# A fused attention and Mish block on one NeuronCore: emission pair by pair on three double PSUM slots, roots on GpSimd, residual seeded into PSUM, smaller first loads

## The chip, the cores and the metric

The kernel runs on one core of one Trainium2 chip. The metric is device time in microseconds (us), the median of several executions; the kernel before takes 204.78 us (204.29 to 205.15 in three runs). The profiler gives a span a little shorter than that time (202.8 us in a run of 204.61 us); all the stage arithmetic below is in the span of the profiled run.

TensorE (PE) multiplies, VectorE (DVE) does statistics, softmax normalisation and half of the casts, ScalarE (ACT) does exponentials, Mish and copies, GpSimd (POOL) has little to do, and SyncE (SP) issues most DMAs. "PEclk" and "clock" are the share of full speed that the throttle granted TensorE.

## The reference

One token block of 2048 x 512. A layernorm feeds two branches: a Hedgehog linear attention (32 heads of 16, feature map by two softmaxes, not causal) and a dense pair with Mish. The sum of the input and both branches is the output.

```python
x  = A_x                                   # 1 x 2048 x 512, bf16
xn = (x - mean) / sqrt(var + 1e-5)
q, k, v = split_heads(xn @ wqkv)           # 32 heads of 16
phi(q)  = concat(softmax(q @ w_phi), softmax(-q @ w_phi))
phi(k)  = concat(softmax(k @ w_phi), softmax(-k @ w_phi))
kv = sum_s phi(k) v ;  z = sum_s phi(k)    # over all 2048 tokens
o  = (phi(q) @ kv) / (phi(q) . z + 1e-6)
h  = xn @ w1 + b1                          # 512 -> 1792
out = x + o @ wo + mish(h) @ w2
```

## The kernel before

The 2048 tokens go through in four groups of 512 (`g`, four tiles of 128). For each group: layernorm and a transpose of it (`xnT`), then `pk` (keys), `pv` (values), `pq` (queries), `pkv` (the sum over tokens) and `ph` (the Mish branch). `w_phi` is folded into the key and query weights on the chip at the start (`fold`: transposes, then matmuls with a block-diagonal matrix, then casts into `wkp` and `wqp`). Since `kv` needs all tokens, an output stage follows all four groups: `pnd` (numerator and denominator), a chain of small VectorE operations, a DMA transpose (`oT`), and `po` (both output matmuls in one PSUM bank).

The parts that the change and the argument touch (cuts marked `# ...`):

```python
    xpool = ctx.enter_context(tc.tile_pool(name="xg", bufs=2))
    xnpool = ctx.enter_context(tc.tile_pool(name="xn", bufs=4))
    xnTpool = ctx.enter_context(tc.tile_pool(name="xnT", bufs=2))
    # ...
    nc.sync.dma_start(xgs[0][:, 0:2, :], x0[:, 0:2, :])
    nc.scalar.dma_start(wk_raw[:], wqkv_v[:, :, D : 2 * D])
    nc.sync.dma_start(xgs[0][:, 2:4, :], x0[:, 2:4, :])
    # ... Wsrc, wv, wq_raw, b1row
    nc.sync.dma_start(w1_sb[:, :, 0:F2], w1_v[:, :, 0:F2])
    nc.sync.dma_start(w1_sb[:, :, F2:F], w1_v[:, :, F2:F])
    xgs[1] = xpool.tile([P, TPG, D], BF16, name="xg")
    nc.sync.dma_start(xgs[1][:], x_g[1])          # x of group 1, behind all of w1
    # ...
    ps_kq = ...tile_pool(name="ps_kq", bufs=2, space=PS)   # two slots of two banks
    ps_v  = ...tile_pool(name="ps_v",  bufs=2, space=PS)   # two banks
    ps_m  = ...tile_pool(name="ps_m",  bufs=2, space=PS)   # two banks

    def stage_ln(g):
        # ...
                    for u in range(t, t + step):
                        nc.vector.bn_stats(st[:], xg[:, u, :])
                        nc.vector.bn_aggr(mv[:, u, :], st[:])
                    chain(nc.scalar.activation(rstd[:, us], mv[:, us, 1], ACT.Sqrt, bias=eps_t[:]))
                    nc.vector.reciprocal(rstd[:, us], rstd[:, us])
                xn = xnpool.tile([P, D], BF16, name="xn")
                nc.vector.tensor_scalar(out=xn[:], in0=xg[:, t, :], ...)
                if g > 0:
                    nc.sync.dma_start_transpose(out=xnT[:, t], in_=xn[:])
                    continue
        # ... (group 0 transposes on TensorE)

    def fold(src, dst):
        # ... transposes of src through ptrw in one bank, ScalarE copies to wT
        for kt in range(KT):
            pf = bank_m("pf")
            for j in range(4):
                nc.tensor.matmul(pf[:, j * P : (j + 1) * P], ...)
            if kt % 2 == 0:
                nc.vector.tensor_copy(dst[:, kt, :], pf[:])
            else:
                nc.scalar.copy(dst[:, kt, :], pf[:])

    # output stage, per group: four nd tiles first, then four output tiles
            y = ypool.tile([P, D], BF16, name="y")
            nc.vector.tensor_tensor(out=y[:], in0=po[:], in1=xg2[:, t, :], op=ALU.add)

    # main order
    fold(wk_raw, wkp)
    fold(wq_raw, wqp)
    for g in range(NG):
        xnT = xnTs[g]
        parts = [stage_kv_pair(xnT, pr) for pr in range(2)]
        stage_q(g, xnT)
        if g + 1 < NG:
            # ... (load of x of group g + 1, for g + 1 > 1)
            xnTs[g + 1] = stage_ln(g + 1)
        stage_kvacc(g, parts)
        acts[g] = stage_h(xnT, apool if g + 1 < NG else apool3)
    for g in range(NG):
        oT = stage_o(g)
        stage_out(g, acts[g], oT)
```

`chain` ties ScalarE's table functions to each other in the order in which they are emitted. On the other engines the source does not fix the order: the instructions are put in an order at compile time.

The softmax here doesn't subtract the row's maximum and nothing guards it: scores larger than these inputs give would overflow.

Of the kernel before, what the change touches and what calls it, by code (L numbers as in the profile page):

```python
# [8 lines left out]
BF16 = mybir.dt.bfloat16  # L9
FP32 = mybir.dt.float32  # L10

ACT = mybir.ActivationFunctionType
ALU = mybir.AluOpType
# [4 lines left out]
def kernel(  # L18
# [50 lines left out]
    x0 = x2[0 : TPG * P].rearrange("(t p) d -> p t d", p=P)  # L69
    nc.sync.dma_start(xgs[0][:, 0:2, :], x0[:, 0:2, :])  # L70
    wk_raw = prep_w.tile([P, KT, D], BF16, name="wk_raw")
    nc.scalar.dma_start(wk_raw[:], wqkv_v[:, :, D : 2 * D])
    nc.sync.dma_start(xgs[0][:, 2:4, :], x0[:, 2:4, :])
    Wsrc = prep_w.tile([P, 4, DH], BF16, name="Wsrc")
    with nc.allow_non_contiguous_dma(reason="tiny w_phi load"):
        nc.scalar.dma_start(Wsrc[:], wphi_v)
# [5 lines left out]
    nc.sync.dma_start(b1row[:], b1_v)  # L82
# [16 lines left out]
    warm = consts.tile([P, 1], FP32, name="warm")  # L99

# [34 lines left out]
    ps_kq = ctx.enter_context(tc.tile_pool(name="ps_kq", bufs=2, space=PS))  # L135
    ps_v = ctx.enter_context(tc.tile_pool(name="ps_v", bufs=2, space=PS))
    ps_m = ctx.enter_context(tc.tile_pool(name="ps_m", bufs=2, space=PS))
# [17 lines left out]
    def big(name):  # L155
        return ps_kq.tile([P, 2, 512], FP32, name=name, tag="kq")

    def bank_v(name):
        return ps_v.tile([P, 512], FP32, name=name, tag="v")

    def bank_m(name, shape=None, dt=FP32):
        return ps_m.tile(shape or [P, 512], dt, name=name, tag="m")


    def stage_ln(g):
        xg = xgs[g]
        mv = spool.tile([P, TPG, nc.vector.BN_AGGR_DIM], FP32, name="mv")
        rstd = spool.tile([P, TPG], FP32, name="rstd")
        xnT = xnTpool.tile([P, TPG, KT, P], BF16, name="xnT")
        step = 1 if g == 0 else TPG  # L170
        for t0 in range(0, TPG, 2):
            ptr = bank_m("ptr", [P, 2, KT, P], BF16) if g == 0 else None
            for t in range(t0, t0 + 2):
                if t % step == 0:
                    for u in range(t, t + step):
                        st = spool.tile([P, nc.vector.BN_STATS_DIM], FP32, name="st")
                        nc.vector.bn_stats(st[:], xg[:, u, :])  # L177
                        nc.vector.bn_aggr(mv[:, u, :], st[:])
                    us = slice(t, t + step)
                    chain(  # L180
                        nc.scalar.activation(
                            rstd[:, us], mv[:, us, 1], ACT.Sqrt, bias=eps_t[:]
                        )
                    )
                    nc.vector.reciprocal(rstd[:, us], rstd[:, us])
                xn = xnpool.tile([P, D], BF16, name="xn")
                nc.vector.tensor_scalar(  # L187
                    out=xn[:],
                    in0=xg[:, t, :],
                    scalar1=mv[:, t, 0:1],  # L190
                    scalar2=rstd[:, t : t + 1],
                    op0=ALU.subtract,
                    op1=ALU.mult,
                )
                if g > 0:
                    nc.sync.dma_start_transpose(out=xnT[:, t], in_=xn[:])
                    continue
                for kt in range(KT):
                    nc.tensor.transpose(  # L199
                        ptr[:, t - t0, kt, :], xn[:, kt * P : (kt + 1) * P], ident[:]  # L200
                    )
            if g == 0:
                nc.scalar.copy(xnT[:, t0 : t0 + 2], ptr[:])
        return xnT
# [12 lines left out]
    def fold(src, dst):  # L217
        wTs = []
        for jh in range(2):
            ptr = bank_m("ptrw", [P, 2, 512], BF16)  # L220
            for jj in range(2):
                j = 2 * jh + jj
                for kt in range(KT):
                    nc.tensor.transpose(
                        ptr[:, jj, kt * P : (kt + 1) * P],
                        src[:, kt, j * P : (j + 1) * P],
                        ident[:],
                    )
            wT = prep_w.tile([P, 2, 512], BF16, name="wT", bufs=2)
            nc.scalar.copy(wT[:], ptr[:])  # L230
            wTs.append(wT)
        for kt in range(KT):
            pf = bank_m("pf")
            for j in range(4):
                nc.tensor.matmul(
                    pf[:, j * P : (j + 1) * P],
                    lhsT=wTs[j // 2][:, j % 2, kt * P : (kt + 1) * P],
                    rhs=Wbd[:, j, :],
                    start=True,
                    stop=True,  # L240
                )
            if kt % 2 == 0:
                nc.vector.tensor_copy(dst[:, kt, :], pf[:])
            else:
                nc.scalar.copy(dst[:, kt, :], pf[:])


    def stage_kv_pair(xnT, pr):
# [12 lines left out]
        chain(nc.scalar.activation(ek[:, 1], pk[:], ACT.Exp, scale=-1.0))  # L261
        v12s = []
# [29 lines left out]
        return ek, v12s  # L292

    def stage_kvacc(g, parts):
        for s0, s1 in ((0, 3), (3, 6), (6, 8)):
            n = s1 - s0
            pkv = bank_m("pkv", [P, n, 8 * VW])
            for s in range(s0, s1):
                pl, j = divmod(s, 4)
                for t in range(TPG):  # L300
                    ek, v12s = parts[t // 2]
                    nc.tensor.matmul(  # L302
                        pkv[:, s - s0, :],
                        lhsT=ek[:, pl, t % 2, j * P : (j + 1) * P],
                        rhs=v12s[t % 2][:, pl, 8 * j : 8 * j + 8, :],
                        start=(t == 0),
                        stop=(t == TPG - 1),
                    )
            if g == 0:
                nc.vector.tensor_copy(kvacc[:, s0:s1, :], pkv[:])  # L310
            else:
                nc.vector.tensor_tensor(
                    out=kvacc[:, s0:s1, :],
                    in0=pkv[:],
                    in1=kvacc[:, s0:s1, :],
                    op=ALU.add,
                )


    def stage_q(g, xnT):  # L320
        gs = slice(g * 512, (g + 1) * 512)
        for jp in range(2):
# [16 lines left out]
    def stage_h(xnT, pool):  # L339
        act = pool.tile([P, FT, 512], BF16, name="act")  # L340
        for fp in range(FT // 2):
# [18 lines left out]
        return act  # L360


    def stage_o(g):
        oT = oTpool.tile([P, TPG, 4, P], BF16, name="oT")
        for t in range(TPG):
            tok0 = g * 512 + t * P
# [49 lines left out]
            nc.sync.dma_start_transpose(out=oT[:, t], in_=o_t[:])  # L416
        return oT

    def stage_out(g, act, oT):
        xg2 = xpool.tile([P, TPG, D], BF16, name="xg")  # L420
        nc.sync.dma_start(xg2[:], x_g[g])
        for t in range(TPG):
            ts = slice(t * P, (t + 1) * P)
            po = bank_v("po")
            for f in range(FT):
                nc.tensor.matmul(  # L426
                    po[:],
                    lhsT=act[:, f, ts],
                    rhs=w2_sb[:, f, :],
                    start=(f == 0),  # L430
                    stop=False,
                )
            for j in range(4):
                nc.tensor.matmul(  # L434
                    po[:],
                    lhsT=oT[:, t, j, :],
                    rhs=wo_sb[:, j, :],
                    start=False,
                    stop=(j == 3),
                )  # L440
            y = ypool.tile([P, D], BF16, name="y")
            nc.vector.tensor_tensor(out=y[:], in0=po[:], in1=xg2[:, t, :], op=ALU.add)  # L442
            nc.sync.dma_start(out_t[g * TPG + t], y[:])
# [7 lines left out]
    fold(wk_raw, wkp)  # L451
    fold(wq_raw, wqp)
    pb = bank_m("pb", [P, FT], BF16)
    nc.tensor.transpose(pb[:], b1row[:], ident[0:FT, 0:FT])
    nc.vector.tensor_copy(b1f[:], pb[:])
    for g in range(NG):
        xnT = xnTs[g]
        parts = [stage_kv_pair(xnT, pr) for pr in range(2)]
        if g == 0:
            prep_w.release()  # L460
            apool3 = ctx.enter_context(tc.tile_pool(name="act3", bufs=1))
            oTpool = ctx.enter_context(tc.tile_pool(name="oT", bufs=2))
            rpool = ctx.enter_context(tc.tile_pool(name="rden", bufs=4))
            opool = ctx.enter_context(tc.tile_pool(name="o_t", bufs=4))
            ypool = ctx.enter_context(tc.tile_pool(name="y", bufs=2))
        stage_q(g, xnT)
        if g + 1 < NG:
# [3 lines left out]
            xnTs[g + 1] = stage_ln(g + 1)  # L471
        stage_kvacc(g, parts)
        acts[g] = stage_h(xnT, apool if g + 1 < NG else apool3)
# [18 lines left out]
    for g in range(NG):  # L492
        oT = stage_o(g)
        stage_out(g, acts[g], oT)


# [28 lines left out]
```

## Time and profile before

| stage of the span (us) | before |
|---|---|
| start to the first transpose | 8.90 |
| first `pk` matmul (the first half of `wkp` is usable) | at 17.78 |
| end of group 0 (first `pk` of group 1) | at 44.46 |
| group 1 | 25.69 |
| group 2 | 25.84 |
| group 3 and output stage, to the last `po` | 103.35 |
| tail | 3.46 |

The head of the page of the kernel before: the span, then busy time per engine, its share of the span and its instructions.

```profile
span 202.8 us, 2765 instructions
...
PE 181.9 (90%) x1041; PEld 89.3 (44%) x1041; DVE 127.7 (63%) x254; ACT 99.6 (49%) x151; POOL 8.6 (4%) x25
```

TensorE binds the kernel. Next, TensorE's waits: who waited for whom, us in total, times, longest.

```profile
PE ptr L199 <- DVE xn L187: 8.9, 1, 8.9
PE ph L346 <- ACT act L356: 1.5, 3, 0.6
PE pq L327 <- ACT ek L261: 1.4, 4, 0.4
PE po L426 <- DVE y L442: 1.1, 1, 1.1
...
PE pf L235 <- DVE wkp L243: 0.8, 1, 0.8
PE pf L235 <- ACT wkp L245: 0.5, 1, 0.5
```

Except for the start, no wait is large; they come to 6.8 us in small pieces. The same span by stage: each row is a stretch, its length, then busy time and instruction counts of each engine, the granted clock, the DMA share and GB/s. The clock is printed as 1.00 where the trace has no clock record, as at the start. The third to fifth rows are groups 1, 2 and 3 up to the first `pnd`, the sixth is the output stage.

```profile
core 0: us, PE busy (x) PEld busy (x) DVE busy (x) ACT busy (x) POOL busy (x), PEclk, DMA share, GB/s
0.00:8.90 8.90, 0.00 (x1) 0.01 (x1) 3.52 (x14) 2.71 (x7) 1.53 (x9) 1.00 0.79 242
8.90:44.46 35.56, 32.72 (x217) 18.35 (x218) 23.53 (x50) 27.13 (x35) 1.83 (x4) 1.00 0.57 177
44.46:70.15 25.69, 24.77 (x137) 12.10 (x136) 16.49 (x28) 20.54 (x26) 1.78 (x4) 1.00 0.17 42
70.15:95.99 25.84, 25.16 (x137) 12.01 (x136) 13.64 (x20) 20.53 (x26) 1.73 (x4) 1.00 0.19 41
95.99:121.94 25.95, 25.58 (x141) 12.26 (x140) 13.76 (x17) 19.07 (x24) 1.74 (x4) 1.00 0.00 1
121.94:199.34 77.40, 73.66 (x414) 34.62 (x412) 56.09 (x127) 9.62 (x34) 0.00 (x0) 1.00 0.27 67
```

A group keeps TensorE "busy" for about 25 of 25.8 us, yet 104 matmuls of 512 columns at the dense step of 0.216 us and 1.9 us of `pkv` make 24.4. The profile models the end of a matmul, so part of the loss hides inside "busy"; a stage is better judged by its length than by its busy share.

### The profile page before, as it was taken

The page shows a single profiled execution, that of the slowest core. Times are in us where ns is not written, and L with a number is a line of the kernel's source. Part 1 is how long each engine was busy: PE and PEld are TensorE (multiplying, and loading weights), DVE is VectorE, ACT ScalarE, POOL GpSimd, SP SyncE. Part 2 cuts the span into 40 slices and gives each one's busy share as a digit, 9 for nine tenths or more (in the row PEclk, how much of TensorE's full clock was granted, in tenths as well). Part 3 has the DMA queues.
Part 4 walks back from the last instruction along what each step waited for, and adds up shares of the span by engine and source line. Part 5 has one row for each costly group of instructions (what it writes and reads, how often), then busy time and mean ns, then how long its engine had stood idle before and what let it go on. Part 6 is the DMA issues. An engine that isn't in the chain of part 4 may idle for free.

```text
span 202.8 us, 2765 instructions
## 1 busy us (share of the span) xinstructions
PE 181.9 (90%) x1041; PEld 89.3 (44%) x1041; DVE 127.7 (63%) x254; ACT 99.6 (49%) x151; POOL 8.6 (4%) x25
## 2 busy tenths in 40 slices
PE   0297998999989999999999999889999999999993
PEld 0264544644446444364444644344444534444440
DVE  0807599916994019950099604893899398848861
ACT  2474999478994789947897373110211011002100
POOL 3000011000110001100011000000000000000000
PEclk9999999999999999999999999999999999999999
DMA  5999600340004400036000000132432262221331
GB/s 174 342 372 348 220 0 2 78 133 0 2 0 81 130 0 0 0 77 132 1 0 0 3 0 0 26 79 81 129 74 55 52 158 53 56 73 26 71 65 50
DMA packets 27321, 15.93 MB, mean 79 GB/s; under 512 B 16300, under 2 KB 27308, under 8 KB 27308
## 3 DMA queue, kind: packets, MB, share of 16 engines
q1 hardware_dynamic: 25724, 14.69, 26.2%
q10 hardware_dynamic: 1584, 1.07, 1.8%
q8 instruction: 8, 0.13, 0.3%
q14 instruction: 5, 0.04, 0.1%
HBM read 9.98 MB, written 2.10 MB: 60 GB/s over the span
## 4 chain that ended last, share of the span: by engine, by line
PE 52%; DMA 17%; ACT 16%; DVE 9%; issue 5%; SPq 0%; ACTq 0%; DVEq 0%
PE ph L346 17%; PE po L426 12%; DMA oT<-o_t 9%; PE po L434 7%; DMA xg<-in_A_x_dram 5%; PE pk L252 4%; PE pkv L302 3%; ACT ek L261 3%; PE pnd L371 3%; PE pq L327 3%; PE pv L266 3%; DMA wk_raw<-in_A_wqkv_dram 2%; ACT eqT L336 2%; ACT ek L260 2%; ACT L356 2%
## 5 line engine op out<-in xcount | busy, mean ns | idle before, releaser
L426 PE MATMUL po<-w_sb,act 128*128 128x512 bf16 x224 | 52.6, 379 | 1.1 <-DVE y L442 1.1
L346 PE MATMUL ph<-xnT,w_sb 128*128 128x512 bf16 x224 | 52.2, 379 | 1.5 <-ACT act L356 1.5
L356 ACT ACTIVATE act<-ph,b1f 128x512 bf16<-128x512 f32 x56 | 35.1, 684 | 18.8 <-PE ph L346 18.8
L384 ACT COPY ds<-pnd 128x64 f32<-128x64 f32 x32 | 8.5, 271 | 59.9 <-PE pnd L371 59.9
L274 DVE TENSOR_REDUCE ss<-ek 128x64 f32<-128x1024 bf16 x16 | 18.7, 1203 | 25.8 <-ACT ek L261 25.8
L426 PEld LDWEIGHTS <-act 128*128 128x128 bf16 x224 | 21.6, 98 | 24.9 <-issue 1.4
L346 PEld LDWEIGHTS <-w_sb 128*128 128x128 bf16 x224 | 21.5, 98 | 24.6 <-issue 2.5
L403 DVE TENSOR_TENSOR on<-pnd,wd 128x512 f32<-128x512 f32 x32 | 20.6, 686 | 1.1
L177 DVE BATCH_NORM_STATS2 st<-xg 128x6 f32<-128x512 bf16 x16 | 10.4, 674 | 14.3 <-DMA xg<-in_A_x_dram 14.3
L442 DVE TENSOR_TENSOR y<-po,xg 128x512 bf16<-128x512 f32 x16 | 10.8, 673 | 12.9 <-PE po L434 12.9
L434 PE MATMUL po<-wo_sb,oT 128*128 128x512 bf16 x64 | 17.8, 380 | 1.2 <-DMA oT<-o_t 0.9
L266 PE MATMUL pv<-wv,xnT 128*128 128x512 bf16 x64 | 17.0, 391 | 0.0
L327 PE MATMUL pq<-xnT,wqp 128*128 128x512 bf16 x64 | 15.1, 378 | 1.4 <-ACT ek L261 1.4
L336 ACT ACTIVATE eqT<-pq 128x1024 bf16<-128x1024 f32 x16 | 15.6, 1036 | 0.6
L252 PE MATMUL pk<-wkp,xnT 128*128 128x512 bf16 x64 | 15.8, 379 | 0.0
L371 PE MATMUL pnd<-kvm,eqT 128*128 128x144 bf16 x128 | 12.9, 227 | 1.4 <-DVE on L403 0.3
L371 PEld LDWEIGHTS <-eqT 128*128 128x128 bf16 x128 | 8.7, 98 | 10.9 <-DVE on L403 9.0
L410 DVE TENSOR_TENSOR o_t<-on 128x512 bf16<-128x512 f32 x16 | 11.1, 692 | 0.6
L302 PEld LDWEIGHTS <-ek 128*128 128x128 bf16 x128 | 8.9, 98 | 5.5 <-DVE v_842 L282 0.6
L388 DVE TENSOR_TENSOR td<-ds 128x64 f32<-128x64 f32 x16 | 3.6, 225 | 11.4 <-ACT ds L384 10.7
L327 PEld LDWEIGHTS <-wqp 128*128 128x128 bf16 x64 | 6.2, 97 | 9.7 <-issue 3.0
L199 PE MATMUL ptr<-ident,xn 128*128 128x128 bf16 x16 | 2.0, 308 | 8.9 <-DVE xn L187 8.9
(101 smaller groups left out, 168.6 us busy)
## 6 DMA issues: line engine op xcount, KB each, us to landing
xg<-in_A_x_dram SPq DMA_DIRECT2D x7, 512.0 KB, 4.4
out_dram<-y SPq DMA_DIRECT2D x16, 128.0 KB, 1.9
w_sb<-in_B_w_dram SPq DMA_DIRECT2D x2, 896.0 KB, 9.1
w_sb<-in_B_w_dram SPq DMA_DIRECT2D x1, 1792.0 KB, 14.7
wk_raw<-in_A_wqkv_dram ACTq DMA_DIRECT2D x1, 512.0 KB, 5.0
xg<-in_A_x_dram SPq DMA_DIRECT2D x2, 256.0 KB, 4.6
wv<-in_A_wqkv_dram SPq DMA_DIRECT2D x1, 512.0 KB, 7.9
wq_raw<-in_A_wqkv_dram ACTq DMA_DIRECT2D x1, 512.0 KB, 8.4
```

The source lines that it names most:

```text
L252: nc.tensor.matmul(pk[:, tt, :], lhsT=xnT[:, 2 * pr + tt, kt, :], rhs=wkp[:, kt, :], start=(kt == 0), stop=(kt == KT - 1),)
L266: nc.tensor.matmul(pv[:], lhsT=xnT[:, 2 * pr + tt, kt, :], rhs=wv[:, kt, :], start=(kt == 0), stop=(kt == KT - 1),)
L274: nc.vector.reduce_sum(ss[:], ek[:, :, tt, :].rearrange("p s (h e) -> p s h e", e=DH), axis=AX.X,)
L302: nc.tensor.matmul(pkv[:, s - s0, :], lhsT=ek[:, pl, t % 2, j * P : (j + 1) * P], rhs=v12s[t % 2][:, pl, 8 * j : 8 * j + 8, :], start=(t = ...
L327: nc.tensor.matmul(pq[:, jj, :], lhsT=wqp[:, kt, j * P : (j + 1) * P], rhs=xnT[:, :, kt, :], start=(kt == 0), stop=(kt == KT - 1),)
L336: chain(nc.scalar.activation(eqT[:, sl, gs], pq[:], ACT.Exp, scale=sign))
L346: nc.tensor.matmul(ph[:, ff, :], lhsT=w1_sb[:, kt, f * P : (f + 1) * P], rhs=xnT[:, :, kt, :], start=(kt == 0), stop=(kt == KT - 1),)
L356: nc.scalar.activation(act[:, f, :], ph[:, ff, :], ACT.Mish, bias=b1f[:, f : f + 1])
L371: nc.tensor.matmul(pnd[:, j // 2, (j % 2) * 144 : (j % 2) * 144 + 144], lhsT=eqT[:, pl * 4 + j, tok0 : tok0 + P], rhs=kvm[:, pl * 4 + j], ...
L403: nc.vector.tensor_tensor(out=on[:, pl], in0=nds[pl][:, :, :, 0:DH], in1=wd[:, pl, :, :, None].to_broadcast([P, 2, 16, DH]), op=ALU.mult,)
L426: nc.tensor.matmul(po[:], lhsT=act[:, f, ts], rhs=w2_sb[:, f, :], start=(f == 0), stop=False,)
L434: nc.tensor.matmul(po[:], lhsT=oT[:, t, j, :], rhs=wo_sb[:, j, :], start=False, stop=(j == 3),)
```

## The change

The intent, in five parts:

1. Smaller first loads: x of group 0 in quarters on two queues, wk in halves, tiny loads on GpSimd's queue.
2. PSUM: three double slots of two banks (before: two double slots and two single banks) and the same two banks for `pv` and `po`. The fold, the transposes and `pkv` use double slots.
3. A set order, pair by pair: `k_pair`, `v_pair`, `q_pair`, `h_pair` interleaved, `nd` two tiles ahead of the output tiles. The fold of wq goes behind the first `k_pair`.
4. The root of groups 1 to 3 on GpSimd as `pow(var + eps, -0.5)`: no Sqrt table loads there.
5. The residual: ScalarE copies x into the `po` bank ahead of the matmuls, which add to it; ScalarE evacuates `po`. VectorE no longer adds x.

```diff
-    nc.sync.dma_start(xgs[0][:, 0:2, :], x0[:, 0:2, :])
-    nc.scalar.dma_start(wk_raw[:], wqkv_v[:, :, D : 2 * D])
-    nc.sync.dma_start(xgs[0][:, 2:4, :], x0[:, 2:4, :])
+    nc.sync.dma_start(xgs[0][:, 0, :], x_t[0])
+    nc.scalar.dma_start(xgs[0][:, 1, :], x_t[1])
+    nc.sync.dma_start(xgs[0][:, 2, :], x_t[2])
+    nc.scalar.dma_start(xgs[0][:, 3, :], x_t[3])
+    nc.sync.dma_start(wk_raw[:, 0:2, :], wk_v[:, 0:2, :])
+    nc.scalar.dma_start(wk_raw[:, 2:4, :], wk_v[:, 2:4, :])
 # ... (Wsrc and b1row to nc.gpsimd.dma_start)
-    ps_kq = ctx.enter_context(tc.tile_pool(name="ps_kq", bufs=2, space=PS))
+    ps_kq = ctx.enter_context(tc.tile_pool(name="ps_kq", bufs=3, space=PS))
     ps_v = ctx.enter_context(tc.tile_pool(name="ps_v", bufs=2, space=PS))
-    ps_m = ctx.enter_context(tc.tile_pool(name="ps_m", bufs=2, space=PS))
 # ...
+    def rstd_of(g, rstd, mv):
+        if g == 0:
+            chain(nc.scalar.activation(rstd, mv, ACT.Sqrt, bias=eps_t[:]))
+            nc.vector.reciprocal(rstd, rstd)
+        else:
+            nc.gpsimd.tensor_scalar(out=rstd, in0=mv, scalar1=1e-5, scalar2=None, op0=ALU.add)
+            nc.gpsimd.tensor_tensor(out=rstd, in0=rstd, in1=mhalf[:], op=ALU.pow)
 # ...
+    def fold_mm(wT, dst):
+        for kp in range(KT // 2):
+            pf = big("pf")
+            for kk in range(2):
+                # ... four matmuls into pf[:, kk]
+            nc.vector.tensor_copy(dst[:, 2 * kp, :], pf[:, 0])
+            nc.scalar.copy(dst[:, 2 * kp + 1, :], pf[:, 1])
 # ... (pkv in two double slots of four heads' blocks, before: three banks)
+        po = bank_v("po")
+        nc.scalar.copy(po[:], x2s[g][:, t, :])            # seed
 # ... (every po matmul start=False)
-            nc.vector.tensor_tensor(out=y[:], in0=po[:], in1=xg2[:, t, :], op=ALU.add)
+        nc.scalar.copy(y[:], po[:])
 # ...
+    wkT = fold_T(wk_raw)
+    fold_mm(wkT, wkp)
     for g in range(NG):
+        if g == 0: wqT = fold_T(wq_raw)
+        ek0 = k_pair(xnT, 0)
+        if g == 0: fold_mm(wqT, wqp)
+        ek1 = k_pair(xnT, 1)
+        v0 = v_pair(xnT, 0, ek0)
+        q_pair(g, xnT, 0); q_pair(g, xnT, 1)
+        h_pair(xnT, acts[g], 0)
+        v1 = v_pair(xnT, 1, ek1)
         # ... load of x and stage_ln of group g + 1
+        for fp in range(1, 4): h_pair(xnT, acts[g], fp)
         stage_kvacc(g, parts)
+        for fp in range(4, 7 if g + 1 < NG else 6): h_pair(xnT, acts[g], fp)
 # ...
+    pos = {0: seed(0), 1: seed(1)}
+    oTs = {0: nd(0)}
+    h_pair(xnTs[NG - 1], acts[NG - 1], 6)
+    oTs[1] = nd(1)
+    for T in range(NT):
+        if T + 2 < NT: oTs[T + 2] = nd(T + 2)
+        out_tile(T, pos[T], oTs[T])
+        if T + 2 < NT: pos[T + 2] = seed(T + 2)
```

## The prediction

> **What bounds the kernel now.** TensorE. The page's first part gives it 181.9 of 202.8 us (90%), VectorE 63%, ScalarE 49%; granted clock 0.998. In the timeline, dense 512-column matmuls step at 0.216 us (34 in 7.34 us), those of 144 and 136 columns at about 0.06. Counting: 704 x 0.216 = 152.1, 128 `pnd` 8.2, 128 `pkv` 7.6, 80 transposes and fold matmuls about 4.9: 173 us of bare issue. The other 30 us, by the timeline:
> - 8.9 us before the first transpose (waits: `ptr` <- `xn` 8.9).
> - 8.9 to 44.5 (fold, group 0): 35.6 us for about 29.2 of issue. The fold ping-pongs on two single banks (`pf` waits for casts of `wkp`); `wkp` is complete only at 18.7.
> - Groups 1 to 3: 25.7 to 25.9 us each for 104 x 0.216 + 1.9 = 24.4. ScalarE holds both double slots (waits `pq` <- `ek`, `ph` <- `act`), with a Sqrt table load and root, 1.28 + 0.30 us, per group.
> - Output stage 122 to 199.4: 77.4 us for 16 x (18 x 0.216 + 8 x 0.064) = 70.4. Waits for `oT` (its transpose takes 2.4 us), for `y` (1.1) and for pnd slots (`on`).
> - 3.4 us of tail.
>
> **What the change does.**
> - First loads in quarters on two queues. `xg` landed at 4.66 and 6.78; I expect about 4 and 5.3. Four statistics at 0.83 us are then the limit; first transpose near 7.9. Gain 1.0.
> - Fold in three double slots: the transposes of wk follow those of xn at once, ScalarE copies (4 x 1.0 us), `wkp` complete near 14.5, the q fold hidden behind k. Group 0 ends near 39.7: a further gain of 3.8.
> - Set order, h_pair 0 and v1 spread between; no Sqrt load in groups 1 to 3. The Trainium skill (ScalarE: Activation LUTs, What ACT_TABLE_LOAD costs) puts a load at 1283 ns plus a drain of 1380; the trace agrees with 1283 but shows no further gap, so I count 1.58 us of ScalarE per group. ScalarE then needs about 20 of 24.4 us. I leave 0.4 us of bubble per group: gain 3.2. The pow on GpSimd is two small operations, off TensorE's path.
> - Output: nd two tiles ahead. The chain pnd, ds, td ... o_t, transpose takes about 7 us against 8.8 of lead. VectorE loses 0.67 us of `y` per tile, leaving about 3.3 of 4.4; ScalarE gains a seed and a copy, about 0.6 each (like the 0.58 cast), and stays below half. The last h pair fills the join. I leave 1.5 us of bubbles: gain 5.4. A matmul adds onto a seed that ScalarE wrote only if an earlier matmul left the bits set (skill: PSUM — Partial Sum Buffer, The four PSUM rules); no run here has shown it yet. It costs no TensorE time.
> - Tail unchanged.
>
> Sum: 1.0 + 3.8 + 3.2 + 5.4 = 13.4; 202.8 - 13.4 = 189.4 span, plus 2 us between span and time: **191.4 us**, range **187.5 to 197**. Faster by over 2%: 0.96; within: 0.03; slower: 0.01.
>
> **What would show it.** First transpose near 7.9; `wkp` complete by 15; three fewer table loads; groups near 24.8; 16 output tiles in about 72 us, no `oT` wait over 0.3; TensorE idle after its start below 6 us.
>
> **What would make it wrong.** The compile-time order may still reorder; pkv now takes double slots, which a busy VectorE could hold 1 to 2 us per group; VectorE's normalisation for the next group, queued behind v1, could deliver xnT late (about 24 us into a group by my estimate); the loads on GpSimd could delay masks; a fuller TensorE could be granted a lower clock.

## More of the kernel before

A line of a timeline has start, duration, engine, line, operation, and in brackets how long the engine was idle before it and what ended that.

```profile
16.22 0.69 DVE L177 BATCH_NORM_STATS2 st<-xg 128x6 f32<-128x512 bf16 x1 [5.62 <-DMA xg<-in_A_x_dram]
16.83 0.67 DVE L243 CAST wkp<-pf 128x512 bf16<-128x512 f32 x1
...
17.78 1.03 PE L252 MATMUL pk<-wkp,xnT 128*128 128x512 bf16 x4
```

A statistic of group 1 (waiting for x of group 1 to land) stands on VectorE ahead of a cast of the fold, although in the source it comes long after it.

## The result, and the profile after

The kernel after takes 198.22 us (197.53 to 198.76 in four runs) against 204.73 for the kernel before. The ratio is 0.968, with a 95% interval of 0.964 to 0.972. Ratios here are the mean time of one kernel's fast runs over that of the other's of the same rounds, so not quite the ratio of the medians that are quoted. Faster by over 2%, as predicted, but by half of the gain that was predicted, and outside the range of 187.5 to 197.

By stage, with what the prediction says or implies (its last group with the output stage is what is left of its 189.4 us):

| stage of the span (us) | before | predicted | after |
|---|---|---|---|
| start to the first transpose | 8.90 | 7.9 | 6.78 |
| `wkp` complete | at 18.8 | about 14.5 | at 21.7 |
| end of group 0 | at 44.46 | about 39.7 | at 46.92 |
| group 1 | 25.69 | about 24.8 | 25.77 |
| group 2 | 25.84 | about 24.8 | 24.34 |
| group 3 and output stage | 103.35 | 96.7 | 96.30 |
| tail | 3.46 | 3.4 | 3.27 |
| span | 202.8 | 189.4 | 196.6 |

So the miss of 7.2 us of span is +7.2 at the end of group 0, +1.0 in group 1, and about -1.0 in the rest. Group 0 ends later than in the kernel before, though its first transpose begins 2.1 us earlier. From `wkp` complete to the end of group 0 the prediction had 25.2 us, and the trace shows 25.2 us: the miss there is all in when `wkp` is complete. That the two agree so closely is in part luck, since this run had a stretch of half clock in there; seven other profiles without one took 24.5 to 24.6 us.

The head of the page after:

```profile
span 196.6 us, 2772 instructions
...
PE 178.5 (91%) x1024; PEld 91.7 (47%) x1041; DVE 117.5 (60%) x232; ACT 110.1 (56%) x177; POOL 14.0 (7%) x33
```

TensorE's waits after:

```profile
PE ptr L207 <- DVE xn L192: 6.8, 1, 6.8
PE pk L260 <- ACT wkp L253: 2.7, 1, 2.7
PE pv L277 <- DVE v_568 L293: 1.0, 1, 1.0
```

The small waits for PSUM slots (`ph`, `pq`, `po`) are gone. One new wait of 2.7 us stands out, of the first `pk` for `wkp`. By stage, from the first transpose on: group 0, groups 1 to 3, and the output stage.

```profile
6.78:46.92 40.14, 34.69 (x216) 19.66 (x218) 27.17 (x60) 25.79 (x33) 5.41 (x10) 0.96 0.60 196
46.92:72.69 25.77, 24.39 (x135) 12.07 (x136) 13.77 (x18) 18.99 (x24) 1.92 (x5) 1.00 0.17 42
72.69:97.03 24.34, 24.23 (x135) 12.09 (x136) 12.20 (x14) 18.99 (x24) 1.75 (x4) 1.00 0.11 22
97.03:119.64 22.61, 22.50 (x127) 11.30 (x128) 13.69 (x16) 18.64 (x24) 1.74 (x4) 1.00 0.00 1
119.64:193.33 73.69, 72.68 (x416) 36.54 (x423) 47.27 (x112) 24.36 (x65) 0.00 (x0) 1.00 0.27 70
```

Group 2 runs at 24.34 us, the bare issue of 24.4 that was counted; group 1 does not. VectorE has 60 instructions in group 0 against 50 before: work of later groups has moved into it. The timeline of the start, and of group 1:

```profile
15.14 1.06 PE L245 MATMUL pf<-Wbd,wT 128*128 128x128 bf16 x12
17.29 1.29 DVE L184 BATCH_NORM_STATS2 st<-xg 128x6 f32<-128x512 bf16 x2 [8.81 <-DMA xg<-in_A_x_dram]
18.57 0.67 DVE L184 BATCH_NORM_STATS2 st<-xg 128x6 f32<-128x512 bf16 x1
19.23 0.67 DVE L184 BATCH_NORM_STATS2 st<-xg 128x6 f32<-128x512 bf16 x1
19.81 1.28 DVE L252 CAST wkp<-pf 128x512 bf16<-128x512 f32 x2
20.52 1.19 ACT L253 CAST wkp<-pf 128x512 bf16<-128x512 f32 x2 [2.77 <-DVE wkp L252]
21.16 2.37 PE L260 MATMUL pk<-wkp,xnT 128*128 128x512 bf16 x8 [2.75 <-ACT wkp L253]
...
47.15 5.12 SPq L202 DMA_TRANSPOSE xnT<-xn  x4
49.70 0.42 DVE L192 TENSOR_SCALAR xn<-xg,mv,rstd 128x512 bf16<-128x512 bf16 x1 [4.08 <-DMA xnT<-xn]
...
54.11 2.34 DVE L285 TENSOR_REDUCE ss<-ek 128x64 f32<-128x1024 bf16 x2
...
58.45 0.81 PE L277 MATMUL pv<-wv,xnT 128*128 128x512 bf16 x3 [1.01 <-DVE v_568 L293]
```

Two things are to be read here.

At the start, the fold's matmuls are done at 16.2. The casts of their results could follow at once, but all four statistics of group 1 stand ahead of them on VectorE. VectorE idles 8.81 us until x of group 1 lands at 17.29 (its load was issued at 5.38, behind the 1.8 MB of w1), spends 2.5 us on the statistics and begins the casts at 19.81. The Trainium skill (PSUM — Partial Sum Buffer, Engine vs sequencer instructions) says that "ScalarE/VectorE/GpSimdE queues are strict FIFO". The trace agrees: two casts that were ready at 16.2 did not pass four statistics that were not, for 3.6 us.

In group 1, the normalisation (`xn`) of group 3 stands on VectorE ahead of the softmax sums (`ss`) of group 1. It needs `xn` buffers (four), which the transposes of group 2 still hold. Those transposes wait for the `xnT` buffer of group 0 (two buffers), which TensorE gives back only as group 0 ends, at 46.9. They run one after the other from 47.15 to about 53.5, the fourth `xn` starts at 53.78, `ss` begins at 54.11, and `pv` waits for its two banks.

### The profile page after: what moved, and what is told of

It is laid out like the page before. It is cut to its first block, busy times and chain, and to the rows that moved or that the text cites. A ratio compares the mean times of both kernels' runs of the same rounds, so it can differ in the third digit from the quotient of the medians.

```text
span 196.6 us, 2772 instructions
## 1 busy us (share of the span) xinstructions
PE 178.5 (91%) x1024; PEld 91.7 (47%) x1041; DVE 117.5 (60%) x232; ACT 110.1 (56%) x177; POOL 14.0 (7%) x33
## 4 chain that ended last, share of the span: by engine, by line
PE 75%; DMA 9%; DVE 7%; SPq 3%; ACT 3%; issue 2%; DVEq 0%
PE ph L353 24%; PE po L439 22%; DMA xg<-in_A_x_dram 7%; PE po L448 6%; PE pk L260 6%; PE pq L335 5%; PE pv L277 5%; PE pkv L313 4%; PE pnd L376 3%; SPq L202 2%; DMA xnT<-xn 1%; DVE st L184 1%; DVE ss L285 1%; DVE on L408 1%; SPq L89 1%
## 5 line engine op out<-in xcount | busy, mean ns | idle before, releaser
L439 PE MATMUL po<-w_sb,act 128*128 128x512 bf16 x216 | 51.2, 379 | 0.4
L353 PE MATMUL ph<-xnT,w_sb 128*128 128x512 bf16 x224 | 50.5, 379 | 0.0
L457 ACT CAST y<-po 128x512 bf16<-128x512 f32 x16 | 9.4, 587 | 44.4 <-PE po L448 44.4
L277 PE MATMUL pv<-wv,xnT 128*128 128x512 bf16 x59 | 16.5, 404 | 2.4 <-DVE v_568 L293 1.0
L260 PE MATMUL pk<-wkp,xnT 128*128 128x512 bf16 x61 | 15.1, 390 | 3.2 <-ACT wkp L253 2.7
L184 DVE BATCH_NORM_STATS2 st<-xg 128x6 f32<-128x512 bf16 x16 | 10.4, 674 | 11.3 <-DMA xg<-in_A_x_dram 11.3
L448 PE MATMUL po<-wo_sb,oT 128*128 128x512 bf16 x63 | 16.4, 379 | 0.1
L335 PE MATMUL pq<-xnT,wqp 128*128 128x512 bf16 x64 | 14.5, 379 | 0.0
L376 PE MATMUL pnd<-kvm,eqT 128*128 128x144 bf16 x128 | 11.3, 226 | 0.5 <-DVE on L408 0.3
L192 DVE TENSOR_SCALAR xn<-xg,mv,rstd 128x512 bf16<-128x512 bf16 x16 | 6.0, 411 | 9.4 <-DMA xnT<-xn 6.9
L260 PEld LDWEIGHTS <-xnT 128*128 128x128 bf16 x64 | 6.4, 100 | 10.6 <-issue 3.6
L277 PEld LDWEIGHTS <-xnT 128*128 128x128 bf16 x64 | 6.4, 102 | 8.2 <-issue 2.0
## 6 DMA issues: line engine op xcount, KB each, us to landing
w_sb<-in_B_w_dram SPq DMA_DIRECT2D x1, 1792.0 KB, 14.3
```

The costliest lines, as they stand in the source:

```text
L184: nc.vector.bn_stats(st[:], xg[:, t, :])
L260: nc.tensor.matmul(pk[:, tt, :], lhsT=xnT[:, 2 * pr + tt, kt, :], rhs=wkp[:, kt, :], start=(kt == 0), stop=(kt == KT - 1),)
L277: nc.tensor.matmul(pv[:], lhsT=xnT[:, 2 * pr + tt, kt, :], rhs=wv[:, kt, :], start=(kt == 0), stop=(kt == KT - 1),)
L335: nc.tensor.matmul(pq[:, jj, :], lhsT=wqp[:, kt, j * P : (j + 1) * P], rhs=xnT[:, :, kt, :], start=(kt == 0), stop=(kt == KT - 1),)
L353: nc.tensor.matmul(ph[:, ff, :], lhsT=w1_sb[:, kt, f * P : (f + 1) * P], rhs=xnT[:, :, kt, :], start=(kt == 0), stop=(kt == KT - 1),)
L376: nc.tensor.matmul(pnd[:, j // 2, (j % 2) * 144 : (j % 2) * 144 + 144], lhsT=eqT[:, pl * 4 + j, tok0 : tok0 + P], rhs=kvm[:, pl * 4 + j], ...
```

## The experiments

All twelve gave correct results. Where a text uses a letter or a short name for a theory, it is one of these:

- **Order on VectorE.** `wkp` is late because statistics of group 1 stand ahead of its casts. Rival: it is late because x of group 1 is loaded too late, and loading it earlier would be enough; or the fold's new PSUM and cast scheme is slow by itself. (Theory Q and Q2 are the order; rival F is the fold by itself.)
- **Order in group 1.** The 1.0 us of group 1 is the hoisted normalisation held by buffers. Rival: it is lower clock or softmax work proper. (Theory B is the buffers; rival G is that group 1 loses time whenever the start is faster.)
- **The other parts.** What seed, pow and first loads are worth. (Theory P is about `pv` matmuls placed ahead of the fold's.)

The experiments that say "order" add an ordering edge between two VectorE instructions. It moves one behind the other in the engine's queue and adds no semaphore and no work:

```python
    def after_on_queue(ins, prev):     # order only
        tc.add_manual_dep(ins.ins, prev.ins.name, DependencyInfo(NoSync, DATA), reason="queue order")
```

The runs came in three batches of four kernels, each with its own runs of the kernel before: 204.59, 204.31 and 204.59 us, and each on another chip. Names of lines shift by a few from kernel to kernel.

A caution for every comparison of starts: in each trace the first matmuls run at half pace (in the kernel after, eight `ptrw` transposes take 1.06 us at 11.72 and 0.61 at 16.04), and the clock record, which sets in where that ends, does so at another moment in each run: at 14.3 in the kernel before, at 15.6 in the kernel after, at 19.3 in the first run below, and between 11.3 and 15.4 in the others. Each kernel has one profile. So a difference of 1 or 2 us in the first `pk` between two of them need not come from the edit alone.

### x of group 1 loaded ahead of w1, in the kernel after

```diff
+    xgs[1] = xpool.tile([P, TPG, D], BF16, name="xg")
+    nc.sync.dma_start(xgs[1][:], x_g[1])
     w1_sb = wts.tile([P, KT, F], BF16, name="w1_sb")
     # ...
-    xgs[1] = xpool.tile([P, TPG, D], BF16, name="xg")
-    nc.sync.dma_start(xgs[1][:], x_g[1])
```

> The kernel after, with one load moved: x of group 1 is issued ahead of the two halves of w1 instead of behind them. Theory Q (VectorE's queue): in the kernel after, three of the four statistics of group 1 stand in VectorE's order ahead of the casts that complete wkp, and they wait for that x, which landed at 17.29 us because 1.8 MB of w1 go first; the casts therefore start only at 19.81 although their matmuls were done at 16.2, and the first pk at 21.16. Q expects x to land near 12, the casts by about 17, the first pk near 17.5 (3.7 us earlier), and the time near 194.7 (3.5 us less than the 198.2 of the kernel after). Rival F (the fold itself, its ScalarE copies and the pv matmuls hoisted into it that wait for wv, bounds the start): the first pk stays within 1 us of 21.2 and the time within 1 us of 198.2.

Measured: 198.26 us (197.73 to 198.66), ratio 0.968 (0.966 to 0.971): no gain. x of group 1 landed by 11.84, 5.5 us earlier, and the first `pk` moved only from 21.16 to 19.97. The timeline of this kernel shows why:

```profile
11.84 1.29 DVE L184 BATCH_NORM_STATS2 st<-xg 128x6 f32<-128x512 bf16 x2 [3.90 <-DMA xg<-in_A_x_dram]
14.64 0.39 DVE L216 TENSOR_TENSOR Wbd<-B16b,Wsrc 128x512 bf16<-128x512 bf16 x1
15.09 0.37 PE L245 MATMUL pf<-Wbd,wT 128*128 128x128 bf16 x2 [3.59 <-DVE Wbd L216]
```

The order on VectorE moved with the load: now the block-diagonal matrix `Wbd` itself came behind the statistics, and the fold's matmuls waited 3.59 us for it. So an earlier load was not enough in the order that the compiler then chose; the run does not test the landing alone, since the order changed as well, and the half pace lasted to 19.3. (The text on record says that three statistics stand ahead of the casts in the kernel after; its trace has all four.)

### The same, in the kernel before

> The kernel before, with the same load moved ahead of w1. Q: there only one statistic stood ahead of the first cast of wkp (cast at 16.83, its matmuls done at about 15.7), so the move gives about 1 us: first pk near 16.8 instead of 17.78, time near 203.7. F: no change (204.7). If it gives 3 us or more, the load bounded the start of the kernel before too, and my prediction misread it as a shortage of banks.

Measured: 203.59 us (202.35 to 204.31), ratio 0.994 (0.989 to 0.999). The first `pk` came at 16.99 instead of 17.78, and the end of group 0 at 43.53 instead of 44.46. The kernel before lost less than 1 us to this wait, because only one statistic stood ahead of a cast there.

### Statistics of group 1 behind the fold's casts, in the kernel after

```diff
-            nc.vector.bn_stats(st[:], xg[:, t, :])
+            b = nc.vector.bn_stats(st[:], xg[:, t, :])
+            if g == 1:
+                after_on_queue(b, last_of["fold"])   # the last VectorE cast of the fold
```

> The kernel after with its loads as they are, but an order-only edge on VectorE: the statistics of group 1 come behind the last cast of the fold (wqp). Q: the casts no longer wait for the load at all; wkp complete near 16.9, first pk near 17.3, group 0 ends near 43 instead of 47.1, time near 194.5. F: first pk within 1 us of 21.2, time within 1 us of 198.2. The statistics of groups 1 to 3 shift together, so group 1 may get slower by up to 1 us on either theory.

Measured: 198.86 us (196.79 to 200.37; one of four runs slow), ratio 0.974 (0.969 to 0.979): no gain in time. The three fast runs alone have a mean of 198.17 us, against 198.18 for the kernel after; the ratio is higher than they give (0.969). Yet in the profiled run, the fastest, group 0 ended near where the prediction had it:

```profile
13.04 1.29 DVE L264 CAST wkp<-pf 128x512 bf16<-128x512 f32 x2 [4.60 <-PE pf L257]
14.40 0.81 PE L272 MATMUL pk<-wkp,xnT 128*128 128x512 bf16 x3 [0.18 <-ACT wkp L265]
15.15 0.60 ACT L265 CAST wkp<-pf 128x512 bf16<-128x512 f32 x1
...
45.05 1.29 DVE L194 BATCH_NORM_STATS2 st<-xg 128x6 f32<-128x512 bf16 x2 [2.08 <-DMA xg<-in_A_x_dram]
...
55.09 3.05 PE L289 MATMUL pv<-wv,xnT 128*128 128x512 bf16 x8 [4.26 <-DVE v L305]
```

The first `pk` starts at 14.40 and group 0 ends at 40.30 (predicted: about 39.7). This settles the first point: the order of VectorE's queue was the cause of most of the loss, 6.0 us at `wkp` complete (15.75 instead of 21.71). It does not show the fold to be as fast as predicted: from the first transpose to `wkp` complete it took 9.0 us, where the prediction had 6.6. An earlier first transpose (by 1.2) and a shorter rest of the group (24.55 for 25.2) make up for most of that.

Then 4.7 of the 6.6 us were given back. Group 1 took 30.45 us instead of 25.77: the statistics of group 3 now waited for x of group 3 (2.08 us idle), ahead of the `ss` of group 1, which began only at 50.74, and `pv` stood for 4.26 us. A repair at one place moved the same fault to the next.

Group 2 then took 24.34 us. The span of this run is 194.7 us, against 196.6 in the kernel after. The mean granted clock was 0.98 to 0.99 in all four runs, and the three at 0.983 took 198.4 us or more; they have no trace, so what they lost besides is not shown.

### More buffers for the normalisation, in the kernel after

```diff
-    xnpool = ...tile_pool(name="xn", bufs=4)
-    xnTpool = ...tile_pool(name="xnT", bufs=2)
+    xnpool = ...tile_pool(name="xn", bufs=8)
+    xnTpool = ...tile_pool(name="xnT", bufs=3)
```

> The kernel after with 8 xn buffers instead of 4 and 3 xnT buffers instead of 2; the order on VectorE is the same. In group 1 of the kernel after (47.1 to 72.9, 25.8 us against 24.3 in group 2), VectorE stood still 6.9 us in all before the normalisations of group 3, which wait for the DMA transposes of group 2, which wait for TensorE to let go of xnT of group 0 at 47.1; the sums ss of group 1 stand behind them and pv waits 1.3 us for v12. Theory B: with the buffers, group 1 takes about 24.4 us, and the time is 1.3 us less, near 196.9; group 0 is unchanged. Rival (group 1 is slow for another reason, such as ScalarE's table load): no change.

Measured: 197.43 us (196.60 to 197.67), ratio 0.964 (0.961 to 0.967). Group 1 went from 25.77 to 24.34 us, and the `xn` of group 3 no longer waited for a transpose; the order of VectorE's instructions stayed the same, by comparison of both kernels' instruction streams. The first `pk` stayed late, at 20.48. So the buffers account for the loss of group 1 in the kernel after, and for nothing of the start.

### Both edges: statistics of group 1 behind the fold, of group 3 behind group 1

```diff
             if g == 1:
                 after_on_queue(b, last_of["fold"])
+            if g == 3:
+                after_on_queue(b, last_of["vm", 1])   # last v12 product of group 1
```

> The kernel after with two order-only edges on VectorE: statistics of group 1 behind the fold (as in the run before), and statistics of group 3 behind the last v12 product of group 1. Theory Q2: the fold edge did what was expected at the start (first pk 14.4 instead of 21.16, group 0 ended at 40.3 instead of 47.1), and the 6.8 us were given back in group 1 (30.4 us instead of 25.8), because VectorE's order had the statistics of group 3 there, waiting for x of group 3 (2.1 us) and for their root and transposes, ahead of the sums ss of group 1, so that pv waited 4.3 us. Q2 expects group 1 at 24.4 to 25, all else as in the run before, time near 190.5 (189.5 to 192). Rival G (group 1 is a slot where time is lost whenever the start is faster, e.g. TensorE or ScalarE bound): group 1 stays above 28 us, time above 194.

Measured: 193.04 us (191.29 to 193.40), ratio 0.943 (0.939 to 0.946). The first `pk` at 16.71, group 0 ends at 42.62, groups 1 and 2 take 24.34 each.

### The fold edge with the buffers instead of the second edge

```diff
             if g == 1:
                 after_on_queue(b, last_of["fold"])
-    # xn bufs=4, xnT bufs=2
+    # xn bufs=8, xnT bufs=3
```

> The fold edge alone, with 8 xn and 3 xnT buffers. The statistics of group 3 still stand ahead of the sums of group 1. Q2: the waits for the transposes go, but the wait for x of group 3 (only two x buffers, the slot is let go late) stays, so the gain is partial: group 1 about 26 to 28 us, time 192 to 195. If buffers were the whole matter in group 1: group 1 at 24.4, time near 190.5.

Measured: 199.34 us (197.59 to 200.79, two of four runs slow), ratio 0.968 (0.964 to 0.972): worse than I had expected. Buffers cannot cure this one: the statistics of group 3 waited for x of group 3 itself (3.22 us idle, until 46.80), group 1 took 29.6 us and `pv` waited 3.7 us for `v`. The buffers help where a buffer is what is waited for (the buffers alone, above), and do nothing where the wait is for a load at the head of the queue.

### Edges for all groups

```diff
             if g == 1:
                 after_on_queue(b, last_of["fold"])
+            if g > 1:
+                after_on_queue(b, last_of["vm", g - 1])
```

> Each group's statistics behind the v12 products of the group before it (the order the program text has). Q2: no hoisting, so no such waits; but statistics, root on GpSimd, normalisation and transposes then end about 24.5 us into each group, where the next group's pk begins: a wait of TensorE for xnT of 0 to 1.5 us at the start of groups 2 and 3. Time 190 to 193. If the hoisting were harmless, this would be no faster than the run with the fold edge alone (198.9).

Measured: 192.60 us (192.01 to 193.44), ratio 0.944 (0.940 to 0.947). By stage: group 0 after the first transpose, groups 1 and 2, and the output stage.

```profile
6.75:41.49 34.74, 32.39 (x215) 18.22 (x218) 20.39 (x40) 25.59 (x33) 3.01 (x6) 1.00 0.56 189
41.49:65.83 24.34, 24.23 (x135) 12.09 (x136) 16.22 (x26) 18.96 (x24) 3.04 (x6) 1.00 0.15 39
65.83:90.18 24.35, 24.24 (x135) 11.96 (x136) 16.10 (x26) 18.96 (x24) 3.00 (x6) 1.00 0.17 44
...
112.93:186.60 73.67, 72.66 (x416) 36.56 (x423) 47.26 (x112) 24.29 (x65) 0.00 (x0) 1.00 0.27 70
```

VectorE now has 40 instructions in group 0 instead of 60, 26 each in groups 1 and 2; the clock record shows 1.00 throughout. The same change, with nothing different but the place of twelve statistics in a queue (and of what hangs on them), is 5.6 us faster.

The span is 189.9 us, where the prediction had 189.4. Part of that agreement is luck, in errors that cancel: the first transpose came 1.2 us earlier than predicted, the rest of group 0 was 2.9 us longer (34.74 for 31.8; `wkp` complete at 16.95), groups 1 and 2 were 0.9 us shorter and what follows 0.4.

### The fold edge in the kernel before

```diff
-                        nc.vector.bn_stats(st[:], xg[:, u, :])
+                        b = nc.vector.bn_stats(st[:], xg[:, u, :])
+                        if g == 1:
+                            after_on_queue(b, last_of["fold"])
```

> The kernel before with the fold edge. There two single banks serve the fold. Reading of my prediction (the fold ping-pongs on two banks): almost nothing, within 0.5 us of 204.7. Q: the first cast at 16.83 waited for x of group 1, so first pk moves from 17.78 to about 16.7 and time falls by about 1 us, to 203.6; the rest of the fold stays bound by the banks.

Measured: 208.51 us (206.75 to 211.39, two of four runs slow), ratio of the fast runs 1.012 (1.008 to 1.016). The first `pk` moved from 17.78 to 15.97:

```profile
14.26 0.50 PE L247 MATMUL pf<-Wbd,wT 128*128 128x128 bf16 x6
14.57 0.69 DVE L255 CAST wkp<-pf 128x512 bf16<-128x512 f32 x1 [4.02 <-PE pf L247]
```

About half of these 1.8 us is the order on VectorE: from these `pf` matmuls to the first `pk` it took 1.7 us here and 2.6 in the kernel before (15.18 to 17.78). The other half was there before any cast: the `pf` matmuls themselves came 0.9 us earlier, in a run whose half pace ended at 12.4 instead of 14.3. TensorE's waits for the two banks fell from 1.3 to 0.3 us. But group 0 ended later, at 46.88:

```profile
35.33 0.30 ACT L193 ACTIVATE rstd<-mv,eps_t 128x4 f32<-128x4 f32 x1 [6.14 <-DVE mv L190]
```

With the root on ScalarE, the late statistics held ScalarE's chain for 6.14 us, and Mish and `ph` behind it. In the kernel before, the layernorm could not be pushed back this far without holding ScalarE. That the `pow` on GpSimd is what makes these edges harmless in the kernel after is likely but not shown: no run has the edges without the pow.

### `pv` of group 0 behind the fold of wk, on top of all edges

```diff
+            # every pv matmul: after_on_queue(m, last_of["pf"])   (last pf matmul of the wk fold)
```

> The run with edges in all groups (192.6 us), plus an order-only edge on TensorE: no pv of group 0 ahead of the wk fold's last matmul. In that run TensorE's order had one pv ahead of the second half of the transposes of wk; it waited 0.7 us for wv to land and then ran at half speed, and five more stood between the fold's matmuls, so that the first pk came at 15.6 to 16.7 (at 14.4 in the one run where wv landed at 9.9). Theory P: first pk near 14.3, and the time falls by 0.7 to 1.5 us, to about 191.5. Rival: the fold is bound by ScalarE's copies of wT and xnT (4 x 1.0 us), the pv only fill holes: no change, or worse by up to 1 us because the pv work is then done later.

Measured: 192.02 us (190.54 to 193.24), ratio 0.937 (0.933 to 0.942). The first `pk` came at 15.34 instead of 15.59, group 0 ended at 41.15 instead of 41.49. The `pv` matmuls that come between the fold's at the start mostly fill holes; what the fold waits for there are ScalarE's copies (0.55 us for `wT`). The difference to the kernel without it is within the spread.

### The seed undone, on top of all edges

```diff
-        nc.scalar.copy(po[:], x2s[g][:, t, :])
...
-                start=False,
+                start=(f == 0),
...
-        nc.scalar.copy(y[:], po[:])
+        nc.vector.tensor_tensor(out=y[:], in0=po[:], in1=x2s[g][:, t, :], op=ALU.add)
```

> The run with edges in all groups, with x added by VectorE as in the kernel before, in place of the seed and the ScalarE copy. My prediction counted this only as relief of VectorE (4.0 instead of 3.3 us of 4.4 per tile): without it VectorE still fits, so at most 1 us slower (192.6 to 193.6). If the seed is what took the waits out of the output stage (before: y held up po 1.1 us, and pnd slots came late because y stood in the way of on), 2 to 4 us slower, with waits of pnd on on.

Measured: 191.77 us (191.12 to 192.24), ratio 0.936 (0.932 to 0.939), the fastest of all, though its difference to the seeded version (192.60, of another batch) is small. Its output stage:

```profile
112.84:186.30 73.46, 72.64 (x416) 36.49 (x423) 56.79 (x127) 10.00 (x36) 0.00 (x0) 1.00 0.27 71
```

73.46 us with VectorE 56.8 us busy, against 73.67 us with the seed and VectorE 47.3 us busy: two tiles take 8.77 us of TensorE either way. The seed takes 9.5 us of work off an engine that was not the limit, and buys nothing.

### The pow undone, in the kernel after

```diff
-        if g == 0:
+        if True:
             chain(nc.scalar.activation(rstd, mv, ACT.Sqrt, bias=eps_t[:]))
             nc.vector.reciprocal(rstd, rstd)
```

> The kernel after (198.2 us) with the roots of groups 1 to 3 on ScalarE again (Sqrt in the table order, between the first and the second pair of Mish, then reciprocal on VectorE). That is 2 table loads and a root, 2.9 us of ScalarE per group, which needs about 20 of 24.4. If that were all, 0 to 3 us slower (198.2 to 201). If the root also ties ScalarE's order to the statistics (as the run of the kernel before with the fold edge hints, where Mish waited for a late root and ph for Mish 2.4 us), some group shows a wait of ph for act of over 1 us.

Measured: 199.00 us (198.82 to 199.28), ratio 0.972 (0.969 to 0.975), about 0.8 us more than the kernel after (of another batch). Group 0 ended 0.7 us later (47.62). Groups 1 and 2 take 25.18 and 25.19 us against 25.77 and 24.34. The table loads are 15 in this kernel, 12 before and 9 after: with the pair-by-pair order, each root costs two loads in the middle of the Mish operations:

```profile
61.10 1.28 ACT L168 ACT_TABLE_LOAD   x1
62.39 0.30 ACT L168 ACTIVATE rstd<-mv,eps_t 128x4 f32<-128x4 f32 x1
62.71 1.28 ACT L363 ACT_TABLE_LOAD   x1
```

Group 2 loses 0.85 us, which I put down to them, and group 1 gains 0.6 us: the root, tied to ScalarE's order, kept the normalisation from running as far ahead as it did on GpSimd (VectorE has 49 instructions in group 0, against 60). At the start it made no difference: all four statistics of group 1 stood ahead of the casts here too, and the first `pk` came at 21.13. That the pow is worth 0.85 us in every group once the order is held in another way is an estimate from group 2; no run tests it.

### The first loads undone, on top of all edges

```diff
+    # the loads from x0 to b1row as in the kernel before
```

> The run with edges in all groups, with the loads up to b1row as in the kernel before (x of group 0 in two halves, wk in one piece on ScalarE's queue, Wsrc and b1row not on GpSimd). The kernel after began its first transpose at 6.78 against 8.90 before, 2.1 us, twice what I predicted. If the loads did that, the first transpose goes back to about 8.9 and the time up by 1.5 to 2.1 us, to about 194.5. If something else did (the order of the statistics), the first transpose stays below 8.

Measured: 192.62 us (192.19 to 193.23), ratio 0.941 (0.938 to 0.944); the version with the small loads has 192.60. In the profiled runs the first transpose came at 8.86 instead of 6.75, the first `pk` at 16.98 instead of 15.59, and the spans are 191.3 and 189.9. So of the 2.1 us at the first transpose 1.4 were left at the first `pk`: with the small loads x landed earlier, but wk was awaited until 8.04 (with the old loads it landed by 5.8) and wv until 10.74 (by 9.2), and TensorE waited for both. This is the order of issue: before, wk was first in ScalarE's queue; now two quarters of x go ahead of it, and half of wk goes ahead of wv. Over all four runs of each the spans overlap, 190.5 to 191.5 with the old loads and 189.9 to 191.3 with the new, and the medians are the same. The mean spans are 191.0 and 190.6; time minus span is 1.7 us with the old loads and 2.1 with the new, which cancels that gain. In time, then, the small loads gained nothing that these runs, of two chips, can show.

## Why the prediction was right or wrong

**Right: what binds the kernel, and that the change gains.** TensorE binds both kernels, and the time fell by over 2%.

**Right at its place, less sure at the end: first transpose.** Predicted 7.9, measured 6.78. The prediction carried its 1.0 us through to the end; undoing the loads cost nothing in the medians, 0.4 us in the mean span and 1.4 us in the profiled spans.

**Wrong, the step that failed: "Fold in three double slots: ... `wkp` complete near 14.5 ... Group 0 ends near 39.7: a further gain of 3.8."** Measured: `wkp` complete at 21.7, end of group 0 at 46.9, a loss of 2.5 us against before where the prediction (with its 1.0 at the start) had a gain of 4.8. The step was wrong in two ways.

First, it left out a wait, and this is most of the miss. What the runs show is the order on VectorE: all four statistics of group 1 stood ahead of the fold's casts and waited for x of group 1. With them behind, `wkp` was complete at 15.75 instead of 21.71, and group 0 ended at 40.30. The prediction's list of risks has "The compile-time order may still reorder", but no stage of the sum has a term for it, and the one statistic ahead of a cast in the trace of before (16.22) was there to be read.

Second, the gain it counted was not there to be had. The reading "the fold ping-pongs on two single banks" took the PSUM banks for the limit, but TensorE waited for them 1.3 us in all, and 0.3 us once the edge was in. The prediction had 6.6 us from the first transpose to `wkp` complete. The seven profiles of the new fold with the edge show 9.0 to 11.3 us; the kernel before took 9.9, and 7.7 with the edge. So no run shows three double slots to be faster than two banks. With all edges, group 0 ended 3.0 us earlier than in the kernel before, not 4.8: 2.1 from the first transpose, nothing from the fold, the rest behind it. What makes the new fold longer than 6.6 us is not settled: wk and wv land later, the half pace at the start varies, and ScalarE's second cast of `wkp` stands behind a copy for wq (1.02 us at 14.24, in the run with the fold edge).

About 0.7 us of the profiled run's excess goes with the clock. The granted clock was 0.50 from 22.4 to 25.8, soon after the 2.75 us wait: the eight `pk` matmuls took 2.37 us, where eight `pv` later took 1.89. From `wkp` complete to the end of group 0 this run took 25.2 us, and so did the run with more buffers, which has the same stop and the same stretch; seven of the eight other variants of the kernel after without it took 24.5 to 24.6 (the eighth, with `pv` moved behind the fold, has that work left to do and took 25.2). The Trainium skill (TensorE: Matmul & The Clock Gate, What's actually happening) describes a default that is throttled, which activity over some 3.4 us releases; that fits the length of the stretch, 3.4 us. In all five kept traces with such a stretch in mid run, it followed a stop of TensorE of 2.75 us or more, and no trace without such a stop at full pace has one. But two runs of the kernel after had a mean clock of 1.0 (spans 195.4 and 195.6); they have no trace, but if they had the same stop, it does not bring the stretch every time, and the run at 0.981 has the same span as the one at 0.991. That the stop caused it is argued, not shown apart.

**Wrong by 1.0 us: group 1.** "I leave 0.4 us of bubble per group": group 1 has 1.4, since the hoisted normalisation of group 3 waited for buffers. Doubling them made the group 24.34 us. The prediction had feared the opposite, a normalisation that comes too late.

**Right: groups 2 and 3, the table loads, the output stage.** Group 2 took 24.34 (predicted 24.8), three fewer table loads (9 for 12). Group 3 with the output stage took 96.30 us (implied: 96.7). The stretch of the sixteen output tiles took 73.7 us; it now holds the last pair of `ph` of group 3, eight matmuls or 1.7 us at 0.216, so the tiles took the predicted 72. No wait for `oT` exceeded 0.2 us. Undoing the pow lengthened group 2 by 0.85 us, less than the 1.58 us of ScalarE per group that the prediction counted, though two loads fell on each root there. The skill (ScalarE: Activation LUTs, What ACT_TABLE_LOAD costs) puts a load at 1283 ns and a drain of 1380 ns. The trace agrees with the first, and shows no gap for the second: the load starting at 61.10 is followed by the root at 62.39.

**Right in outcome, but not for its reason: the seed.** The result is right with a seed that ScalarE wrote. The skill (PSUM — Partial Sum Buffer, The four PSUM rules) says that such a write neither sets nor clears the bits that decide between adding and overwriting, and that a matmul adds to the seed where they are set, as they are after an earlier matmul wrote there; all runs with the seed were correct, in banks that `pv` had written in full before. But VectorE was not the limit of the output stage, and undoing the seed cost nothing (191.77 us against 192.60). By exclusion, the gain of the output stage comes from `nd` two tiles ahead and the filled join; I did not undo these alone, so that is argued.

**Not explained.** Time minus span is 2.0 to 2.2 us in the kernel after and most variants, 1.7 to 1.8 with the pow or the loads undone, and 1.7 to 1.9 in the kernel before and its variants; the prediction took 2. Also open is why ScalarE's first cast of `wkp` starts only as VectorE's first ends (20.52 after 19.81, also 13.76 after 13.04), although they read different banks.

The whole account: 189.4 + 7.2 (group 0) + 1.0 (group 1) - 1.0 (groups 2, 3, output, tail) = 196.6 us of span. With the order held, 189.9, in part by errors that cancel.

## What to carry to other kernels

Emitting work in a set order sets TensorE's order only if nothing holds it; on VectorE, look in the trace for an instruction that waits for a load and stands ahead of a cast that the critical path needs, and count it as a term of the sum. Work for later groups can be placed one or two groups early by the compiler, up to the point where it blocks on a load or a buffer; with the root of the layernorm on GpSimd it ran further ahead here than with the root on ScalarE. Where it blocks on a load, an ordering edge helped here (192.60 us) and more buffers did not (199.34). And after a repair, read the same trace again at the next stage before believing the gain: one edge gained 6.6 us by the end of group 0 and nothing in the mean of its fast runs, all edges together gained 5.6. Before more buffers are given to a stage, sum what it waits for the ones it has: here the fold's waits came to 1.3 us, where a gain of 3.8 was predicted.

## What the Trainium skill lacked or had wrong

- ScalarE: Activation LUTs, What ACT_TABLE_LOAD costs: the drain of about 1380 ns per load was not seen here as idle time; the load of 1.28 us at 61.10 is followed by the next operation at 62.39.
- No page that I found gives the cost of `pow` on GpSimd: here 1.04 us for 128 x 4 values, and 0.23 us for the add before it.
- PSUM — Partial Sum Buffer, Engine vs sequencer instructions states the strict order of the queues, but as a matter of reading traces. What it costs is not there: here a statistic that waited for a load held two casts for 3.6 us, and in another variant `pv` for 4.26 us.
